# Attention, routed experts and a second attention on one core: the head of the first stage in another order, with filler matmuls

## The chip, the cores and the metric

One core of a Trainium2 chip runs one program: TensorE, VectorE, ScalarE and GpSimd compute, SyncE (SP) issues most of the DMAs. The metric is the device time of one execution in microseconds, lower is better; what stands for a kernel is the median of several executions.

## The reference, cut to what matters

Three stages in a row. The change touches the head of the first one only.

```
def _attn_ref(q, k, v, proj):                 # q, k, v: (2, 8, 768, 64), proj: (64, 6)
    scale = 1.0 / np.sqrt(D)
    q_bits = (np.einsum('bhsd,dk->bhsk', q, proj) > 0).astype(np.int64)
    k_bits = (np.einsum('bhsd,dk->bhsk', k, proj) > 0).astype(np.int64)
    powers = 2 ** np.arange(n_bits)
    q_bucket = np.sum(q_bits * powers, axis=-1)
    k_bucket = np.sum(k_bits * powers, axis=-1)
    mask = q_bucket[:, :, :, None] == k_bucket[:, :, None, :]
    scores = scale * np.matmul(q, k.transpose(0, 1, 3, 2))
    scores = np.where(mask, scores, -1000000000.0)
    scores = scores - np.max(scores, axis=-1, keepdims=True)
    attn = np.exp(scores)
    attn = attn / (np.sum(attn, axis=-1, keepdims=True) + 1e-09)
    return np.matmul(attn, v).astype(np.float32)

x = attention of all heads, (2, 768, 512)
x = _moe_ref(x, ...)      # each row through one of 8 experts, 512 -> 1024 -> 512
return _moe2_ref(x, ...)  # 4 experts that are causal attentions, the best 2 of each row
```

## The kernel before, in words

The first stage (`stage_a`) works on eight units, each a pair of heads of one batch, so that 128 partitions hold both heads or one head twice. For a unit it loads q and k transposed, makes their hash bits with a small matmul and a comparison, and builds wide operands `QM` and `KM`: rows 0 to 23 the bits, row 32 the row maxima of the scores (against ones on the side of k), rows 64 to 127 a rounded copy of q or k. One matmul of `KM` with `QM` so gives masked scores. What rounding lost is in `Q1` and `K1`, a second matmul.

Steps are small functions. Those of the head:

- `load(u, n)`: DMA of one head's q or k (n = 0 q of head 0, 1 k of head 0, 2 q of head 1, 3 k of head 1). In unit 0 it brings 64 partitions (192 KB), and `load2(n)` the same data to the other 64; in later units it brings 128 partitions (384 KB). `loadp(u, w)`: q (w = 0) or k (w = 1) of both heads, for the bits of units 1 to 7. `loadv(u)`: v. `proj`, `consts`: constants.
- `split(u, n)`: ScalarE rounds q or k into `QM`, `KM`. `split2(u, n)`: ScalarE rounds it into `Q1`, `K1`, and another engine subtracts to get the rest.
- `bits0(h, c, w)` (unit 0): matmul on TensorE, comparison on VectorE straight into `QM` or `KM`. `bits(u)` (other units): four matmuls, one comparison on VectorE; `qbits` and `kbits` then write the result into place on ScalarE.
- `mx(u, qh, n)`: one of twelve score matmuls of half qh, and its maximum on VectorE. `mneg`: the twelve to six. `mrow`: a transpose on TensorE, an eviction on VectorE and a DMA on SP (L287) that writes row 32.
- `score(u, x, h)`: two matmuls into one of three PSUM buffers `sc`, and the exp on ScalarE. `av`, `padd`, `sums`, `norm`, `rows1` to `rows3` follow. `warm(i, n)`: n filler matmuls whose result nobody reads. `fixed(i)`: memsets on GpSimd.

Each step is added to a plan with its dependences and costs of a planner (`at`, `ops`, in ns; those of bits of unit 0 are `("PE", 640, "S"), ("DVE", 660)`). The costs don't act when the kernel is built: `pl.run(ORDER_A)` calls the steps in the order of a list of numbers, and every engine and queue runs its instructions in just that order; waits come from the data. Eight fillers run ahead of the list. A PSUM pool `mx` of three buffers serves the bits, the maxima and the transposes.

The order written out, engine by engine, up to the first scores:

```
before
SP       load(0,1) proj proj load(0,2) load(0,3) load(0,0) load2(1) loadp(1,0) load(1,1) load2(3) consts load2(0)
         load(1,2) load(1,0) load2(2) loadp(1,1) load(1,3) mrow(0,0) loadv(0) loadp(2,1)
TensorE  bits0 x6, mx(0,0,.) x12, warm(1,2), bits(1), mrow(0,0), bits0 x2, warm(0,2), mx(0,1,.) x3,
         score(0,1,0) score(0,0,0) mx score(0,0,1) mx score(0,1,1)
VectorE  bits0 x6, mx x12, mneg, bits(1), mrow(0,0), bits0 x2, mx(0,1,.)
ScalarE  split(0,1) (0,3) (0,2) (0,0), split2(0,1) (0,0), split(1,1) (1,0), split2(0,3), split(1,3), split2(0,2),
         qbits(1,1), kbits x3, exp of score(0,1,0)
GpSimd   fixed(1) zeros fixed(0) identity, ones in pt, fill_table, subtractions of split2(0,1) (0,0) (0,3) (0,2)
```

Of the kernel before, what the change touches and what calls it, by code (L numbers as in the profile page):

```python
# [126 lines left out]
def stage_a(tc, ctx, g, q, k, v, pb):  # L127
    nc = tc.nc
# [101 lines left out]
    def split2(u, n):  # L230
        h, w = divmod(n, 2)
        X1 = (Q1, K1)[w][u % NB][:, h, :]
        x = st[u]["x"][w, h]
        lo = slice(64 * w, 64 * w + 64)
        nc.scalar.activation(X1, x, AF.Copy)
        e = nc.vector if u else nc.gpsimd
        e.tensor_sub(X1[lo], x[lo], X1[lo].bitcast(F32))
# [195 lines left out]

    def xout(kk, k):
        if kk + k == 0:
            sb.xt[0] = [sb.rp.tile([128, 4, CAP], F32R, name=f"x0{n}") for n in "hl"]
        h, l = (a[:, 2 * kk + k, :] for a in sb.xt[0])
        x = st["xt", kk][:, k, :]
        nc.scalar.activation(h, x, AF.Copy)
        nc.vector.tensor_sub(l, x, h.bitcast(F32))  # L440
# [15 lines left out]
    X = range(2)  # L456
    T = range(NKT)
    for n in X:
        add(proj, n, at=(-30.9, -29.4)[n], ops=dma(182), tail=900)
# [16 lines left out]
    for u in range(NU):  # L476
        b, p = units[u]
# [6 lines left out]
        for n in range(4):  # L484
            dep = [(f, u - 2, m) for f in ("split", "split2") for m in range(4)]
            dep += [("bits0", h, c, w) for w in X for c in X for h in X] if u == 2 else []
            add(load, u, n, at=o - 31 + 1.5 * n, ops=dma(1092 if u else 546), deps=dep + now(o - 31 + 1.5 * n) if u > 1 else [],
                tail=900)
            if u == 0:
                add(load2, n, at=-25 + n, ops=dma(546), deps=[("load", 0, n)], tail=900)  # L490
            add(split, u, n, at=o - 21 + n + 7 * (u == 1), ops=[("ACT", 740)], deps=[("load", u, n)] + seen)
            add(split2, u, n, at=o - 20 + n + 8 * (u == 1), ops=[("ACT", 735), ("DVE", 920, "p") if u else ("Pool", 1800, "p")],
                deps=[("load", u, n) if u else ("load2", n)] + used + [("mrow", 0, 0)] * (u == 1))
# [3 lines left out]
        for c in X:  # L497
            if u:
                add(loadp, u, c, at=o - 28 + c, ops=dma(1092), deps=([("bits", u - 1)] if u > 1 else []) + now(o - 28 + c) * (u > 1),
                    tail=900)  # L500
            else:
                for h in X:
                    for w in X:
                        add(bits0, h, c, w, at=-2 + h if c > w else -10 + 2.4 * h + .4 * (c + w), ops=[("PE", 640, "S"), ("DVE", 660)], bank="mx",
                            deps=[("load", 0, 2 * h + w), ("proj", 0), ("proj", 1)] + [("mneg", 0, 0)] * (c > w))
        if u:
            add(bits, u, at=o - 20 + 6 * (u == 1), ops=[("PE", 640, "Q"), ("DVE", 470)], bank="mx",
                deps=[("loadp", u, w) for w in X] + [("mneg", 0, 0)] + ([(f, u - 1, *x) for f, x in MOVES] if u > 1 else []))
# [8 lines left out]
        for qh in X:  # L517
            z = 2 * u + qh
            last = lambda f, n=2: [(f, *divmod(z - n, 2))] if z >= n else []
            for n in range(12):  # L520
# [4 lines left out]
                    + ([("mneg", u - 2, y) for y in X] if u > 1 else []), bank="mx")  # L525
# [4 lines left out]
            for kt in T:  # L530
# [7 lines left out]
                for h in X:  # L538
                    add(score, u, x, h, at=o + x + .4 * h, ops=[("PE", 349), ("ACT", 373)],
                        deps=[("mrow", u, qh)] + free + [("warm", i, 2) for i in X if u + qh == 0] + [(f, u, 2 * h + w) for f in ("split", "split2") for w in X] + bdep,  # L540
# [40 lines left out]
    u = NU - 1  # L581
# [1001 lines left out]
```

## Time and profile before

| | us |
|---|---|
| median of three executions | 607.95 (605.28 to 609.09) |
| the profiled execution, its own time | 608.14 |
| its span, first to last instruction | 606.4 |
| TensorE busy in the span | 579.6 (96%) |
| VectorE, ScalarE, GpSimd busy | 443.1, 369.8, 252.1 |

The first stage takes the span's first 250 us or so. Times in the profile count from the start of the span. A busy TensorE is not one at its peak, as its matmuls overlap. "A <- B" in a wait means that A's instruction waited for B's. The clock column is the granted clock of TensorE, 1.00 for 2.4 GHz and 0.50 for 1.2 GHz.

### The profile page before, as it was taken

What the parts mean: (1) busy time and instruction counts of PE and PEld (TensorE: products, weight loads), DVE (VectorE), ACT (ScalarE), POOL (GpSimd) and SP (SyncE); (2) the same over time, 40 slices, a digit from 0 to 9 for tenths busy, and PEclk for the clock granted to TensorE, in tenths of its full rate; (3) what the DMA queues carried; (4) which work ended last, traced back from release to release, by engine and by line L of the source; (5) the groups of instructions that cost most, each with busy time, mean ns of one, the idle gap of its engine ahead of it and who ended that gap; (6) DMA issues with size and microseconds to landing.
All of it is one profiled execution on the core that took longest, in us unless ns stands there. A gap on an engine that the chain in (4) does not pass through costs nothing. (4 is left out here: it accounts for less than half of the span.)

```text
span 606.4 us, 9769 instructions
## 1 busy us (share of the span) xinstructions
PE 579.6 (96%) x3537; PEld 448.8 (74%) x3537; DVE 443.1 (73%) x853; ACT 369.8 (61%) x676; POOL 252.1 (42%) x256
## 2 busy tenths in 40 slices
PE   8999989999899999899999999999989999998995
PEld 3556657767576675798898998997969878787573
DVE  6699888988889798756656776755444576787872
ACT  4999878989695476154545545544537565554541
POOL 7696577686767784620000000000044024653840
PEclk8999999999999999899999999999999999999998
DMA  8535347265425415247656757665555010210222
GB/s 230 206 130 174 119 151 261 75 225 157 166 62 174 120 56 183 89 138 250 242 176 248 243 198 242 220 233 174 177 166 155 18 28 15 66 27 2 54 105 104
DMA packets 53718, 88.81 MB, mean 146 GB/s; under 512 B 3860, under 2 KB 26512, under 8 KB 53408
## 3 DMA queue, kind: packets, MB, share of 16 engines
q1 hardware_dynamic: 51712, 81.78, 41.3%
q0 software_dynamic: 1952, 6.34, 3.3%
q8 instruction: 29, 0.48, 0.4%
q14 instruction: 25, 0.20, 0.1%
HBM read 66.18 MB, written 20.26 MB: 143 GB/s over the span
## 5 line engine op out<-in xcount | busy, mean ns | idle before, releaser
L320 POOL TENSOR_TENSOR acc<-acc,pt 128x768 f32<-128x768 f32 x56 | 110.6, 1977 | 43.0 <-ACT pt L298 40.6
L274 DVE TENSOR_REDUCE m<-mp 128x1 f32<-128x384 f32 x192 | 96.4, 548 | 10.0 <-PE mp L273 9.2
L298 ACT ACTIVATE pt<-sc 128x384 f32<-128x384 f32 x192 | 85.5, 486 | 24.1 <-PE sc L297 21.1
L1079 POOL DMA_INDIRECT xg<-ys,slot x12 | 12.2, 1018 | 193.4 <-DVE wl L1049 185.7
L850 DVE TENSOR_TENSOR wlo<-wraw,whi 128x1024 fp32r<-128x1024 f32 x64 | 76.3, 1231 | 12.3 <-ACT whi L849 12.2
L307 PE MATMUL av<-pt,vt 128*64 128x385 f32 (+1 forms) x384 | 70.7, 493 | 0.0
L273 PE MATMUL mp<-km,qm 128*128 128x384 f32 x192 | 65.3, 379 | 5.4 <-DVE m L274 3.6
L849 ACT ACTIVATE whi<-wraw 128x1024 fp32r<-128x1024 f32 x64 | 64.4, 1053 | 9.0 <-DMA wraw<-in_w_dram 5.3
L295 PE MATMUL sc<-qm,km 128*128 128x384 f32 x192 | 67.6, 352 | 1.2 <-ACT pt L298 0.6
L297 PE MATMUL sc<-q,k 128*128 128x384 f32 x192 | 64.6, 336 | 0.0
L889 PE MATMUL hp<-xth,whi 128*128 128x256 f32 x224 | 63.0, 281 | 1.7 <-PEq L1017 1.7
L890 PE MATMUL hp<-xtl,whi 128*128 128x256 f32 x224 | 62.9, 281 | 0.0
L891 PE MATMUL hp<-xth,wlo 128*128 128x256 f32 x224 | 62.8, 280 | 0.0
L273 PEld LDWEIGHTS mp<-km,qm 128*128 128x128 f32 x192 | 35.6, 192 | 25.1 <-DVE m L274 10.6
L907 PE MATMUL yp<-whi,hh 128*128 128x512 f32 x128 | 51.5, 402 | 0.0
L908 PE MATMUL yp<-wlo,hh 128*128 128x512 f32 x128 | 50.4, 393 | 0.0
L909 PE MATMUL yp<-whi,hl 128*128 128x512 f32 x128 | 50.3, 393 | 0.0
L307 PEld LDWEIGHTS av<-pt,vt 128*64 128x64 f32 x384 | 25.4, 136 | 32.1 <-issue 28.8
L894 ACT ACTIVATE hh<-hp 128x512 fp32r<-128x512 f32 x32 | 19.1, 598 | 45.0 <-PE hp L891 44.9
L1281 POOL TENSOR_TENSOR cp<-cp,cp 128x384 f32<-128x384 f32 (+2 forms) x50 | 39.5, 812 | 17.0 <-PE cav L1273 16.1
L889 PEld LDWEIGHTS hp<-xth,whi 128*128 128x128 f32 x224 | 42.1, 188 | 2.4 <-issue 2.1
L895 DVE SCALAR_TENSOR_TENSOR hl<-hp,hh 128x512 fp32r<-128x512 f32 x32 | 22.0, 688 | 28.4 <-ACT hh L894 28.4
(263 smaller groups left out, 1387.6 us busy)
## 6 DMA issues: line engine op xcount, KB each, us to landing
wraw<-in_w_dram SPq DMA_DIRECT2D x32, 1024.0 KB
xs<-zt SPq DMA_DIRECT2D x13, 512.0 KB
x<-in_k_dram SPq DMA_DIRECT2D x14, 384.0 KB
x<-in_q_dram SPq DMA_DIRECT2D x14, 384.0 KB
xsb<-xs SPq DMA_DIRECT2D x7, 512.0 KB
ys<-ysb SPq DMA_DIRECT2D x7, 512.0 KB
vt<-in_v_dram SPq DMA_DIRECT2D x8, 384.0 KB
xp<-in_q_dram SPq DMA_DIRECT2D x7, 384.0 KB
```

The source lines that it names most:

```text
L273: nc.tensor.matmul(mp, QM[i][:, o:o + 128], KM[i][:, h * S + c * HS:h * S + (c + 1) * HS], start=True, stop=True)
L274: nc.vector.tensor_reduce(s["m"][:, qh, h, t, c:c + 1], mp, axis=AX.X, op=ALU.max)
L295: nc.tensor.matmul(sc, KM[i][:, h * S + kt * 128:h * S + kt * 128 + 128], QM[i][:, (2 * qh + h) * HS:(2 * qh + h + 1) * HS], start=True, s ...
L297: nc.tensor.matmul(sc, K1[i][:, h, ks], Q1[i][:, h, qs], start=False, stop=True)
L298: nc.scalar.activation(PT[(u * 12 + x) % NPB][:, h, :HS], sc, AF.Exp, scale=SCALE)
L307: nc.tensor.matmul(s["av", qh][64 * h:64 * h + 64, :HS + 1 - qh], s["v"][:, h, kt, :], P[:, h, :HS + 1 - qh], start=kt == 0, stop=kt == NK ...
L320: (nc.vector if u == NU - 1 else nc.gpsimd).tensor_add(s["acc", qh], p, P)
L849: nc.scalar.activation(hi[:, s], r[:, s], AF.Copy)
L850: nc.vector.tensor_sub(lo[:, s], r[:, s], hi[:, s].bitcast(F32))
L889: nc.tensor.matmul(p[:, f2, :], hi, xh[:, k, :], start=k == 0, stop=False)
L890: nc.tensor.matmul(p[:, f2, :], hi, xl[:, k, :], start=False, stop=False)
L891: nc.tensor.matmul(p[:, f2, :], lo, xh[:, k, :], start=False, stop=k == 3)
```

## The change

The list ORDER_A has a new beginning; its last 945 steps are the same steps in the same order. The first unit's eight loads and the constants are issued first. The transpose of the first row of maxima (`mrow(0,0)`) and its DMA come before the second unit's bits, and the second unit's loads come behind that DMA on SP. Thirteen steps `hwarm` put filler matmuls between the bits of the first unit (three, three) and between its first twelve maxima (one each). `warm(0)` and `warm(1)` have three fillers instead of two. Two of the first unit's four subtractions go from GpSimd to VectorE, behind the row.

```
after
SP       load(0,1) proj proj load(0,0) load(0,3) load(0,2) load2(1) load2(0) load2(3) load2(2) consts
         mrow(0,0) loadp(1,0) loadp(1,1) load(1,0) load(1,1) load(1,2) load(1,3) loadv(0) loadp(2,1)
TensorE  bits0(0,0,1) (0,1,1), 3 fillers, bits0(0,0,0) (1,0,1) (1,1,1), 3 fillers, bits0(1,0,0),
         mx(0,0,0) filler mx(0,0,1) filler ... mx(0,0,11), mrow(0,0), 6 fillers, bits(1), bits0 x2, mx(0,1,.) x3,
         score(0,1,0) score(0,0,0) mx score(0,0,1) mx score(0,1,1)
VectorE  bits0 x6, mx x12, mneg, mrow(0,0), subtractions of split2(0,3) (0,2), bits(1), bits0 x2, mx(0,1,.)
ScalarE  split(0,1) (0,0) (0,3) (0,2), split2(0,1) (0,0) (0,3) (0,2), split(1,1) (1,0) (1,3),
         qbits(1,1), kbits x3, exp of score(0,1,0)
GpSimd   fixed(0) identity, ones in pt, fixed(1) zeros, subtractions of split2(0,1) (0,0), fill_table
```

The code of it, cut to its core:

```
-        e = nc.vector if u else nc.gpsimd
+        e = nc.vector if u or h else nc.gpsimd
         e.tensor_sub(X1[lo], x[lo], X1[lo].bitcast(F32))
...
+    def hwarm(i, n):
+        warm(i, n)
+
...
+    for i, n in enumerate((3, 3) + (1,) * 11):
+        add(hwarm, i, n, at=-8, ops=[("PE", 213 * n)], deps=[("mx", 0, 0, i - 4)] if i > 3 else [], bank="sc")
...
-            add(load, u, n, at=o - 31 + 1.5 * n, ops=dma(1092 if u else 546), deps=dep + now(o - 31 + 1.5 * n) if u > 1 else [],
+            add(load, u, n, at=o - 31 + 1.5 * n, ops=dma(1092 if u else 700), deps=dep + now(o - 31 + 1.5 * n) if u > 1 else [("load2", y) for y in range(4)] * u,
                 tail=900)
             if u == 0:
-                add(load2, n, at=-25 + n, ops=dma(546), deps=[("load", 0, n)], tail=900)
+                add(load2, n, at=-25 + n, ops=dma(700), deps=[("load", 0, y) for y in range(4)], tail=900)
...
-                            deps=[("load", 0, 2 * h + w), ("proj", 0), ("proj", 1)] + [("mneg", 0, 0)] * (c > w))
+                            deps=[("load", 0, 2 * h + w), ("proj", 0), ("proj", 1)] + [("mrow", 0, 0)] * (c > w))
         if u:
             add(bits, u, at=o - 20 + 6 * (u == 1), ops=[("PE", 640, "Q"), ("DVE", 470)], bank="mx",
-                deps=[("loadp", u, w) for w in X] + [("mneg", 0, 0)] + ([(f, u - 1, *x) for f, x in MOVES] if u > 1 else []))
+                deps=[("loadp", u, w) for w in X] + [("mrow", 0, 0)] + ([(f, u - 1, *x) for f, x in MOVES] if u > 1 else []))
...
+                    + ([("hwarm", n + 1, 1)] if u + qh == 0 and n else []), bank="mx")
...
-        add(warm, i, 2, at=-3 + .3 * i, ops=[("PE", 850)], deps=[("mx", 0, 0, 11)], bank="sc")
+        add(warm, i, 3, at=-3 + .3 * i, ops=[("PE", 640)], deps=[("mx", 0, 0, 11)], bank="sc")
```

The dependences of the plan (`deps`) only say which orders are allowed; the order is the list's.

## Rows read from the trace of the kernel before

**Rows 1.** Busy times by stretch: engines, then granted clock, DMA share, GB/s.

```profile
20.00:30.00 10.00, 9.32 (x48) 6.68 (x47) 8.12 (x18) 9.83 (x17) 7.42 (x8) 1.00 0.66 238
```

**Rows 2.** Waits from 22 to 255 us: total, times, longest.

```profile
ACT pt L298 <- PE sc L297: 21.1, 40, 2.0
...
PEld sc L295 <- DMA qm<-mr: 0.9, 1, 0.9
```

**Rows 3.** Timeline of ScalarE: start, duration, instruction, idle before and releaser.

```profile
18.12 0.84 ACT L227 ACTIVATE km<-x 64x768 fp32r<-64x768 f32 x1 [0.71 <-DMA x<-in_k_dram]
18.99 0.84 ACT L235 ACTIVATE q<-x 128x768 fp32r<-128x768 f32 x1
19.86 1.03 ACT L258 ACTIVATE qm<-bt,cstt 24x768 fp32r<-24x768 f32 x1
...
22.82 2.19 ACT L298 ACTIVATE pt<-sc 128x384 f32<-128x384 f32 x5
```

**Rows 4.** Timeline of the SP queue: start and duration of the issue.

```profile
11.58 0.33 SPq L164 DMA_DIRECT2D x<-in_k_dram  x1
19.07 0.88 SPq L287 DMA_DIRECT2D qm<-mr  x1
20.00 0.39 SPq L184 DMA_DIRECT2D vt<-in_v_dram  x1
...
22.60 0.91 SPq L164 DMA_DIRECT2D x<-in_k_dram  x2
```

**Rows 5.** Waits of the SP queue in the first 30 us.

```profile
SPq L287 <- DVE mr L286: 7.1, 1, 7.1
```

**Rows 6.** Timeline of VectorE.

```profile
5.30 1.32 DVE L253 TENSOR_SCALAR km<-bp,cstt 32x384 fp32r<-32x384 f32 x2 [4.15 <-PE bp L251]
...
9.68 5.64 DVE L274 TENSOR_REDUCE m<-mp 128x1 f32<-128x384 f32 x12
15.36 0.17 DVE L280 TENSOR_REDUCE mn<-m 128x6 f32<-128x12 f32 x1
...
18.72 0.27 DVE L286 TENSOR_SCALAR mr<-mtp 6x128 fp32r<-6x128 f32 x1
```

**Rows 7.** Timeline of TensorE in the head.

```profile
17.20 1.00 PE L243 MATMUL bp<-xp,pbt 128*32 128x384 f32 x4 [0.22 <-DMA xp<-in_k_dram]
18.13 0.27 PE L284 MATMUL mtp<-ident,mn 128*6 128x128 f32 x1
...
23.33 0.44 PE L295 MATMUL sc<-qm,km 128*128 128x384 f32 x1 [0.63 <-ACT pt L298]
```

**Rows 8.** Busy times by stretch, with the granted clock, around the first maxima.

```profile
10.90:17.60 6.70, 6.48 (x16) 2.69 (x18) 4.59 (x11) 3.36 (x4) 2.86 (x3) 0.50 0.99 310
```

**Rows 9.** Busy times by stretch, read for the last column, GB/s.

```profile
17.00:18.00 1.00, 0.80 (x4) 0.19 (x4) 0.00 (x0) 0.41 (x1) 0.51 (x1) 0.72 0.27 101
20.00:21.00 1.00, 0.96 (x5) 0.44 (x3) 1.00 (x3) 0.99 (x2) 1.00 (x1) 1.00 0.01 3
21.00:28.00 7.00, 6.37 (x34) 5.12 (x33) 5.54 (x13) 6.89 (x12) 5.87 (x7) 1.00 0.93 336
34.00:36.00 2.00, 2.00 (x12) 1.99 (x12) 1.68 (x4) 1.97 (x5) 1.87 (x2) 1.00 1.03 403
```

**Rows 10.** Busy times and granted clock where the first stage ends.

```profile
252.00:258.00 6.00, 5.31 (x29) 4.85 (x30) 3.33 (x17) 0.60 (x2) 4.15 (x9) 0.72 0.23 89
254.00:256.00 2.00, 2.00 (x9) 1.64 (x8) 0.94 (x8) 0.00 (x0) 0.72 (x1) 0.50 0.34 131
```

**Rows 11.** Timeline of TensorE near 252 us and near the end.

```profile
252.69 0.50 PE L428 MATMUL sc<-q,qm 128*128 128x256 f32 x2 [2.01 <-DVE q L423]
...
258.13 1.90 PE L1455 MATMUL sc<-onesb 128*128 128x512 bf16 x8
...
598.54 0.63 PE L1330 MATMUL cop<-wh,cxl 128*128 128x512 f32 x1
598.97 0.63 PE L1328 MATMUL cop<-wh,cah 128*128 128x512 f32 x1
```

More of the change, by code (lines that the diff above doesn't have):

```diff
@@ L486, in stage_a @@
             dep += [("bits0", h, c, w) for w in X for c in X for h in X] if u == 2 else []
-            add(load, u, n, at=o - 31 + 1.5 * n, ops=dma(1092 if u else 546), deps=dep + now(o - 31 + 1.5 * n) if u > 1 else [],
+            add(load, u, n, at=o - 31 + 1.5 * n, ops=dma(1092 if u else 700), deps=dep + now(o - 31 + 1.5 * n) if u > 1 else [("load2", y) for y in range(4)] * u,
                 tail=900)
             if u == 0:
-                add(load2, n, at=-25 + n, ops=dma(546), deps=[("load", 0, n)], tail=900)
+                add(load2, n, at=-25 + n, ops=dma(700), deps=[("load", 0, y) for y in range(4)], tail=900)
             add(split, u, n, at=o - 21 + n + 7 * (u == 1), ops=[("ACT", 740)], deps=[("load", u, n)] + seen)
-            add(split2, u, n, at=o - 20 + n + 8 * (u == 1), ops=[("ACT", 735), ("DVE", 920, "p") if u else ("Pool", 1800, "p")],
-                deps=[("load", u, n) if u else ("load2", n)] + used + [("mrow", 0, 0)] * (u == 1))
+            add(split2, u, n, at=o - 20 + n + 8 * (u == 1), ops=[("ACT", 735), ("DVE", 920, "p") if u or n > 1 else ("Pool", 1800, "p")],
+                deps=[("load", u, n) if u else ("load2", n)] + used + [("mrow", 0, 0)] * (u == 1) + [("mneg", 0, 0)] * (u == 0 and n > 1))
         add(loadv, u, at=o - 20, ops=dma(1092), deps=[("av", u - 3, x) for x in range(12)] if u > 2 else now(o - 20) if u > 1 else [],
@@ L498, in stage_a @@
             if u:
-                add(loadp, u, c, at=o - 28 + c, ops=dma(1092), deps=([("bits", u - 1)] if u > 1 else []) + now(o - 28 + c) * (u > 1),
+                add(loadp, u, c, at=o - 28 + c, ops=dma(1092), deps=([("bits", u - 1)] + now(o - 28 + c) if u > 1 else [("load2", y) for y in range(4)]),
                     tail=900)
@@ L524, in stage_a @@
                     + ([("bits0", h, qh, 0), ("bits0", h, n % 2, 1)] if u == 0 else [])
-                    + ([("mneg", u - 2, y) for y in X] if u > 1 else []), bank="mx")
+                    + ([("mneg", u - 2, y) for y in X] if u > 1 else [])
+                    + ([("hwarm", n + 1, 1)] if u + qh == 0 and n else []), bank="mx")
             e = o - 6 + 6 * qh if u else 3.1 * qh - 3.2
@@ L539, in stage_a @@
                     add(score, u, x, h, at=o + x + .4 * h, ops=[("PE", 349), ("ACT", 373)],
-                        deps=[("mrow", u, qh)] + free + [("warm", i, 2) for i in X if u + qh == 0] + [(f, u, 2 * h + w) for f in ("split", "split2") for w in X] + bdep,
+                        deps=[("mrow", u, qh)] + free + [("warm", i, 3) for i in X if u + qh == 0] + [(f, u, 2 * h + w) for f in ("split", "split2") for w in X] + bdep,
                         bank="sc")
```

88 rows, old and new, of the table ORDER_A are left out of this document.

## The prediction

> **What bounds the kernel now.** I read five views, in this order. First the busy times by stretch: from 20 to 30 us ScalarE is busy 9.83 of 10 us and TensorE 9.32 [rows 1], so once the attention stage runs there is no room in which a late start could be made good. Second, the waits from 22 us to the end of that stage: engines wait for each other (ScalarE for the scores, 21.1 us in all), and the only wait of a computing engine for a DMA is 0.9 us for a row of maxima; none is for a load of q or k [rows 2]. A delay that all engines have after the head therefore reaches the end whole. Third, ScalarE's timeline: the last part of the second unit that is read from memory is copied at 18.12 (it waited 0.71 us for the DMA of k), one more copy of the first unit follows at 18.99, the second unit's bits at 19.86, and the first exp only at 22.82 [rows 3]. The head ends at this exp: TensorE has three buffers for scores, and its fourth score pair, at 23.33, waits for it [rows 7]. Fourth, the SP queue, which issues in program order: the second unit's last load leaves at 11.58, then the queue stands 7.1 us before the DMA of the first row of maxima, because that needs VectorE's result, and only at 20.00 does the next load leave [rows 4, 5]. Fifth, why the row is late: VectorE has the maxima ready at 15.53 (15.36 + 0.17) [rows 6], but the transpose that makes the row stands on TensorE behind the second unit's bits, which wait for k until 17.20; it runs at 18.13 and the DMA leaves at 19.07 [rows 4, 7].
>
> **The change part by part.** What may be gained: the row no longer stands behind the second unit's bits. What is paid: the second unit's six loads now stand behind the row's DMA on SP, and ScalarE needs three of them, the last one among them, before the first exp.
>
> *The first row of maxima.* VectorE's first piece still starts at 5.30, as the first load and the two constants keep their places. Six evictions of bits at 0.66 (two take 1.32) are followed by twelve maxima in 5.64, 0.47 each [rows 6]. The fillers, three each before the third and the sixth piece of bits, cost at the full clock at most 0.24 each (eight in 1.90) [rows 11], 0.7 a time. With 0.64 for a piece of bits on TensorE (the cost in the code): the third is done at 5.74 + 0.7 + 0.64 = 7.1 where VectorE was free at 6.6, the sixth at about 9.7 where VectorE was free at 9.2. Two gaps of about 0.5 to 0.65, so the evictions end at 10.45 and the maxima at 16.1; before they ended at 15.3. The loads that come sooner gain nothing here, since each of the pieces had its data by then. Between maxima, one filler and one maximum's matmul take 0.24 x (1 + 384/512) = 0.42 at the full clock, under VectorE's 0.47: no cost. The row then needs the reduction 0.17, the transpose 0.27, the eviction 0.27 and some 0.1 for each handover [rows 6, 7]: the DMA leaves at 17.05 instead of 19.07. That is the whole gain, 2.0 us. It can't be much more: with no gap the evictions and maxima take 4.0 + 5.64 from 5.30, and the DMA leaves at 15.9.
>
> *The second unit's loads.* All six wait on SP until the row's DMA is issued. That takes 0.88 [rows 4], so the first goes out at 17.95. Before, a load issued at 20.00 had moved next to nothing by 21.0 (3 KB in that us), and from 21 to 28 us six loads of 0.393 MB, 2.36 MB, were moved at 336 GB/s, 2.35 MB [rows 4, 9]. That stretch had gaps between the issues (20.00 to 23.5); issued back to back at 0.46 (two in 0.91 [rows 4]) the rate should be nearer to the 403 GB/s of 34 to 36 us [rows 9]. Six loads take 7.0 us by the one and 5.85 by the other; I take 6.2, nearer to the back-to-back rate. First data at 17.95 + 1.15 = 19.1, last at 25.3. Before, data stopped some 0.27 us after 17 us (101 KB at about 380 GB/s) and the copy that waited for it started at 18.12 [rows 3, 9], so I add 0.85: the copy starts at 26.15. The first unit's copies are all done by then, so the second unit's bits follow at once, at 27.0, where they ran at 19.86 [rows 3]: **+7.15 us**. From there to the first exp ScalarE's order is unchanged (2.96 us from the one row to the other), so it starts at 30.0 instead of 22.82. The bounds: DMA at 15.9, 5.85 us of transfer and a tail of 0.7 give +4.9; with 7.0 us and a row 0.5 later, +8.5.
>
> The Trainium skill puts a DMA at about 2.0 us fixed plus bytes over 436 GB/s ("DMA: Bandwidth & Descriptors", Anatomy of one DMA; a fit for GpSimd's queue). For one stream of these bytes that would be an estimated 7.4 us from issue to landing where my rows give 8.2, and a time 0.8 us lower. The same page's Rules for kernel authors say to issue early and wait late, which this change does the other way round for the second unit.
>
> *What TensorE does meanwhile.* The second unit's bits stand ahead of all scores on TensorE and need the first two loads, landed at about 19.1 + 2.0 + 0.85 = 22. So TensorE is idle from about 18.3 (the six fillers behind the row) to 22, then runs the bits, seven matmuls and three score pairs, and is idle again from about 26.5 until 30.5. Before, after an idle time of 2.0 us that ended at 252.7, the granted clock was at 0.50 in 254 to 256 [rows 10, 11]; at that level a 512-column matmul takes 0.43 (two starts, 598.54 and 598.97) instead of at most 0.24 [rows 11]. If the clock is low where the scores restart, TensorE, which has no room there, loses up to half of that stretch: 1.7 us for a drop as long as that one (a mean of 0.72 over 6 us is 3.4 us at 0.50 [rows 10]), 0 if it stays high or falls in the idle time. I take **+0.5**.
>
> The Trainium skill describes a kernel whose waits for DMA let the clock fall at every round ("TensorE: Matmul & The Clock Gate", HAM oscillation). By it the fall would be sure and the time 1.2 us above my sum.
>
> *The rest.* Two of the four subtractions of the first unit move from GpSimd to VectorE behind the row, where VectorE waits for the second unit's bits anyway until 23; the first unit's last copies move ahead on ScalarE, which waits until 24 anyway; the memsets change places on GpSimd, whose first result is needed at about 9.7 and ready at 5: nothing on the path. If the loads did not cover them, the subtractions would be about 2 us on VectorE. The v load is seventh, lands at about 27.2 and is needed at about 32.5. The remaining 945 steps keep their order.
>
> **Sum.** 608.14 us (the profiled execution: its span 606.4 and 1.7 around it) + 7.15 + 0.5 = **615.8 us**. The median shown, 607.95, lies 0.2 below that execution.
>
> **The rivals.**
> *The first row is slowed by its own fillers.* Before, the clock was at 0.50 from 10.9 to 17.6 [rows 8], through most of the maxima. If it is so again, a matmul of 384 columns and a filler take 0.32 + 0.43 = 0.75 instead of 0.47, and the twelve maxima 9.0 instead of 5.64; where half of them see the low clock, 1.7 more. For it: the low stretch is there in the trace. Against it: the fillers are just what keeps TensorE denser than before. All that follows shifts by it: 617.5 to 619.
> *The loads come faster or part of the delay is made good.* With the lower bounds above, +4.9 gives 613.0; with 2 us made good by waits that I have overlooked in the stage, 611 to 613.5.
> *The loads are not held back, and the 2.0 us are kept* (the other side). If the SP queue let the loads go when they are reached in the list, before the row's DMA, they would start at about 8 us, behind the first unit's 1.6 MB, and all be there by about 16, as before by 18. The first exp would then follow the row: 608.14 - 2.0 = 606.1. It decides when the sixth load has landed by about 17.9, two us before the bits' 19.86. Against it speaks the queue's own row: 7.1 us of standing before the row's DMA with loads queued behind it [rows 5], and loads that leave in just the order of the list. That would also be the case where the change doesn't do what I read in it.
>
> **How the numbers follow.** Chances: 0.50 for my sum (613.5 to 617.5), 0.22 for slow maxima, 0.20 for the smaller delay, 0.08 for no delay. The predicted time is the first one's, 615.8. The range leaves out the last case and the end of the second: 611.0 to 620.0. About 1%, 6.1 us, is what a measurement of this kernel can tell from no change; three runs lay between 605.28 and 609.09. Slower by more than that means over 614.0: nearly all of slow maxima and somewhat under 0.9 of the first case with the scatter of the runs, less a little: 0.69. Faster needs under 601.9, which no case gives: 0.03. The rest is 0.28.
>
> **What would show it.** In the changed trace: on SP a load of k or q leaving right behind the row's DMA at about 18, none of the second unit before; ScalarE waiting some 9 to 13 us for loads of k and q, with the last wait ending near 26; the first exp near 30; TensorE with two idle stretches of 3 to 4 us before 31; the row's DMA near 17. From then on every landmark (the last exp of the stage, the first expert's matmul) some 7 to 8 us later than before. I am wrong if the second unit's loads are issued before the row, if ScalarE's copies precede 22 us, or if the shift shrinks on the way to the end.

## The result and the profile after

The changed kernel takes 617.81 us (median of four executions, 615.78 to 620.1) against 608.52 for the kernel before: ratio 1.0144, 95% interval 1.0103 to 1.0184. Measured once more beside the kernels of the experiments, it takes 618.45 (four executions, 614.99 to 621.83) against 607.65, ratio 1.0171 (1.011 to 1.0231). The forecast was 615.8, within 611 to 620, slower. The execution that was profiled took 615.78 against 608.14, with a span of 614.0 against 606.4.

The row's DMA leaves earlier, as it was meant to, and the second unit's loads go out behind it. The SP queue of the changed kernel (timeline, then its longest wait), to be read against [rows 4, 5]:

```profile
7.53 0.62 SPq L205 DMA_DIRECT2D cstt<-in_cst_dram  x1
17.24 0.88 SPq L287 DMA_DIRECT2D qm<-mr  x1
18.17 0.39 SPq L179 DMA_DIRECT2D xp<-in_q_dram  x1
...
20.50 0.57 SPq L164 DMA_DIRECT2D x<-in_k_dram  x1
21.11 0.53 SPq L184 DMA_DIRECT2D vt<-in_v_dram  x1
...
SPq L287 <- DVE mr L286: 9.0, 1, 9.0
```

The queue stands 9.0 us before the row's DMA with nothing in flight for the second unit; the sixth load leaves at 20.50 where it left at 11.58. VectorE shows why the row is no sooner than 17.24 (its timeline, against [rows 6]): two gaps, 0.84 and 0.18, where TensorE runs fillers ahead of the third and the sixth piece of bits, then the twelve maxima at the old pace.

```profile
5.54 1.32 DVE L253 TENSOR_SCALAR km<-bp,cstt 32x384 fp32r<-32x384 f32 x2 [4.40 <-PE bp L251]
7.70 0.66 DVE L253 TENSOR_SCALAR qm<-bp,cstt 32x384 fp32r<-32x384 f32 x1 [0.84 <-PE bp L251]
...
9.87 0.67 DVE L253 TENSOR_SCALAR qm<-bp,cstt 32x384 fp32r<-32x384 f32 x1 [0.18 <-PE bp L251]
10.57 5.66 DVE L274 TENSOR_REDUCE m<-mp 128x1 f32<-128x384 f32 x12
```

ScalarE pays (its timeline, against [rows 3]): it is done with the first unit at 12.2, stands 13.44 us until k of the second unit has landed, once more 0.37 for the last load, and starts the first exp at 31.38 instead of 22.82.

```profile
11.36 0.85 ACT L235 ACTIVATE q<-x 128x768 fp32r<-128x768 f32 x1
25.64 0.84 ACT L227 ACTIVATE km<-x 64x768 fp32r<-64x768 f32 x1 [13.44 <-DMA x<-in_k_dram]
...
27.57 0.84 ACT L227 ACTIVATE km<-x 64x768 fp32r<-64x768 f32 x1 [0.37 <-DMA x<-in_k_dram]
28.43 1.02 ACT L258 ACTIVATE qm<-bt,cstt 24x768 fp32r<-24x768 f32 x1
...
31.38 1.21 ACT L298 ACTIVATE pt<-sc 128x384 f32<-128x384 f32 x3
32.95 0.49 ACT L298 ACTIVATE pt<-sc 128x384 f32<-128x384 f32 x1 [0.36 <-PE sc L297]
33.91 0.49 ACT L298 ACTIVATE pt<-sc 128x384 f32<-128x384 f32 x1 [0.47 <-PE sc L297]
```

The last two rows show the second, smaller loss: ScalarE now waits for scores. Busy times by stretch, with granted clock, DMA share and GB/s in the last three columns, against [rows 9, 10]:

```profile
20.00:22.00 2.00, 0.79 (x4) 0.14 (x4) 0.00 (x0) 0.00 (x0) 0.00 (x0) 0.91 1.14 341
22.00:24.00 2.00, 1.39 (x6) 0.19 (x4) 0.00 (x0) 0.00 (x0) 0.00 (x0) 0.50 0.78 229
24.00:26.00 2.00, 1.86 (x6) 0.19 (x4) 0.67 (x2) 0.36 (x1) 0.00 (x0) 0.50 1.04 410
...
34.00:36.00 2.00, 2.00 (x9) 1.16 (x7) 1.38 (x3) 1.96 (x4) 1.35 (x1) 0.68 0.00 0
...
252.00:258.00 6.00, 5.80 (x47) 4.90 (x47) 5.39 (x30) 1.24 (x4) 1.59 (x3) 1.00 0.22 82
```

The clock is at 0.50 from 21.6 us until 35.3, over the first 3.9 us of exps, and the loads have a slack stretch of 229 GB/s at 22 to 24 us.

How the delay goes on can be read from landmarks. The row of `mneg` (sixteen in the stage: count, shortest, median and longest in ns, first and last start) in the kernel before and in the changed one:

```profile
L280 DVE TENSOR_REDUCE mn<-m x16: 125/155/166, 15.4 to 216.6; 128x6 f32<-128x12 f32 x16
```

```profile
L280 DVE TENSOR_REDUCE mn<-m x16: 126/156/168, 16.3 to 226.6; 128x6 f32<-128x12 f32 x16
```

The first exp is 8.6 us late, the last `mneg` 10.0. Nothing is made good from the first exp to there. Behind it 2.4 us come back in this pair of executions (the spans differ by 7.6): the kernel before had its clock down in 252 to 258 us (0.72 [rows 10]), the changed one nowhere between its last `mneg` and its last 20 us. What follows the last `mneg` goes with that clock in all fourteen profiles: 386.5 to 389.0 us in the seven without such a fall, 388.6 to 390.5 in the five with one or two falls of 3.4 us, 391.8 and 392.8 in the two with 10 us at the low level. Whether the changed kernel has fewer of these falls than the kernel before, or had so by chance, stays open. The medians differ by 9.3.

### The profile page after: what moved, and what is told of

It reads as the page before. It is cut to its first block, busy times and chain, and to the rows that moved or that the text cites. A ratio compares the mean times of both kernels' runs of the same rounds, so it can differ in the third digit from the quotient of the medians.

```text
span 614.0 us, 9808 instructions
## 1 busy us (share of the span) xinstructions
PE 583.2 (95%) x3556; PEld 450.8 (73%) x3556; DVE 443.7 (72%) x855; ACT 370.1 (60%) x676; POOL 250.4 (41%) x254
## 5 line engine op out<-in xcount | busy, mean ns | idle before, releaser
L1287 POOL TENSOR_TENSOR cp<-cp,cp 128x384 f32<-128x384 f32 (+2 forms) x50 | 39.5, 812 | 16.9 <-PE cav L1279 15.2
L896 PEld LDWEIGHTS hp<-xtl,whi 128*128 128x128 f32 x224 | 42.1, 188 | 0.2
```

The costliest lines, as they stand in the source:

```text
L896: nc.tensor.matmul(p[:, f2, :], hi, xl[:, k, :], start=False, stop=False)
```

## The experiments

Four theories. A: the second unit's loads, held on SP behind the row's DMA, are the loss. B: the fillers, or the clock, are. C: the two subtractions on VectorE delay the second unit's bits. D, against a part of the prediction: the row was not what ended the head of the kernel before, so its 2 us are worth nothing.

The kernels change the order by a small function ahead of the run:

```
    def moved(order, steps, mark):              # these steps right ahead of that one
        keys = list(pl.items)
        ids = [keys.index(s) for s in steps]
        order = [n for n in order if n not in ids]
        at = order.index(keys.index(mark))
        return order[:at] + ids + order[at:]
```

What all of them showed, by profile: when the row's DMA left on SP, when the first exp and the last `mneg` started (in parentheses how much later than in the kernel before), and the time as a ratio to the kernel before.

| kernel | loads held | row's DMA | first exp | last mneg | ratio (95%) |
|---|---|---|---|---|---|
| before | 0 | 19.07 | 22.82 | 216.6 | |
| row ahead of the bits alone (e3) | 0 | 16.99 | 22.69 (-0.1) | 216.6 (0) | 1.001 (0.9987 to 1.0033) |
| loads ahead, no fillers (e8) | 0 | 16.95 | 23.76 (0.9) | 217.5 (0.9) | 1.0013 (0.998 to 1.0046) |
| e8, bits sooner (e10) | 0 | 17.11 | 23.41 (0.6) | 217.5 (0.9) | 1.0009 (0.9985 to 1.0034) |
| e8, bits among the maxima (e9) | 0 | 19.13 | 23.07 (0.3) | 217.2 (0.5) | 0.9999 (0.9966 to 1.0032) |
| loads ahead (e1) | 0 | 22.47 | 27.88 (5.1) | 221.6 (5.0) | 1.0011 (0.9977 to 1.0045) |
| two held, no fillers (e12) | 2 | 16.51 | 25.42 (2.6) | 219.2 (2.6) | 1.0056 (1.0025 to 1.0087) |
| two held (e6) | 2 | 17.09 | 25.82 (3.0) | 219.6 (3.0) | 1.0126 (1.0072 to 1.018) |
| no fillers (e2) | 6 | 16.42 | 30.21 (7.4) | 225.8 (9.2) | 1.0148 (1.0098 to 1.0198) |
| changed | 6 | 17.24 | 31.38 (8.6) | 226.6 (10.0) | 1.0144 (1.0103 to 1.0184) |
| changed, again (e13) | 6 | 23.76 | 37.98 (15.2) | 231.8 (15.2) | 1.0171 (1.011 to 1.0231) |
| last two exchanged (e4) | 6 | 22.62 | 36.16 (13.3) | 230.4 (13.8) | 1.0141 (1.0093 to 1.0189) |
| more fillers in the idle time (e5) | 6 | 17.91 | 31.87 (9.1) | 227.1 (10.5) | 1.0207 (1.0116 to 1.0298) |
| e2, first unit's exps first (e11) | 6 | 17.98 | 23.21 (0.4) | 232.1 (15.5) | 1.0231 (1.018 to 1.0281) |

**Loads ahead of the row's DMA (e1).**

```
+    order = moved(ORDER_A, [("loadp", 1, 0), ("loadp", 1, 1), ("load", 1, 0), ("load", 1, 1), ("load", 1, 2), ("load", 1, 3)], ("fixed", 0))
```

> The changed kernel with one thing undone: the second unit's six loads are issued right behind the constants, ahead of the first row's DMA; the fillers, the row ahead of the bits and the moved subtractions stay. Theory A (the loads held on SP behind the row's DMA are the cost): ScalarE's wait of 13.4 us for k shrinks to below 6 us, the second unit's bits follow the two subtractions on VectorE, the first exp starts near 22.7 instead of 31.4, and the time is that of the kernel before within 2 us (606 to 610). Theory B (the fillers, or the low clock that follows them, are the cost): the time stays above 614. Theory C (the two subtractions on VectorE delay the bits): a rest of 1 to 2 us against the kernel before stays.

608.55 us against 606.63: the loss is gone, as far as the interval tells, with the loads back in front, while all fillers and the moved subtractions stay. Five of its ten executions lie between 605.9 and 607.4, as the kernel before does; the others reach up to 615.29. ScalarE's wait for k fell to 3.65 us. A holds, B is out as the main cause. The first exp of the profiled execution (612.38) was not at 22.7, though, but at 27.88, since here the row's DMA left only at 22.47 and the second unit's bits stand behind it; more on that below. ScalarE of this kernel:

```profile
15.94 0.84 ACT L227 ACTIVATE km<-x 64x768 fp32r<-64x768 f32 x1 [3.65 <-DMA x<-in_k_dram]
...
24.92 1.03 ACT L258 ACTIVATE qm<-bt,cstt 24x768 fp32r<-24x768 f32 x1 [6.21 <-DVE bt L245]
```

**No fillers among bits and maxima (e2).**

```
     def hwarm(i, n):
-        warm(i, n)
+        pass
```

> The changed kernel without the seventeen fillers among the first bits and maxima (the six behind the row stay). Theory A: the maxima end 0.6 to 1.2 us sooner, the row's DMA and the loads behind it leave as much sooner, the first exp comes near 30.5 instead of 31.4; the time stays 6.5 to 9 us above the kernel before. Theory B: the time falls to within 2 us of the kernel before. Should the clock be at 0.50 during the maxima as in the kernel before, VectorE still sets their pace at 0.47.

Row at 16.42, first exp at 30.21, 616.25 us: still 9.6 us above the kernel before. As A expected, the fillers are 0.8 us of the row and 1.2 us of the first exp in this pair of profiles.

**The row ahead of the second unit's bits, in the kernel before (e3).**

```
+    order = moved(ORDER_A, [("mrow", 0, 0)], ("bits", 1))
```

> The kernel before with one part of the change: the transpose and DMA of the first row of maxima come ahead of the second unit's bits; loads, fillers and subtractions as before. Theory A, in the form of the prediction (the row is worth what its DMA gains): the row's DMA leaves at 16.4 instead of 19.07 and the time falls by 2 us or more. Theory D (the row was not last: ScalarE's copies and bits of the second unit set the first exp at 22.8 in any case): the row's DMA leaves as much sooner, the first exp stays at 22.8 within 0.3, and the time stays within 1 us of the kernel before.

The row's DMA leaves 2.1 us sooner, and the first exp moves by 0.1. From the SP queue and ScalarE of this kernel:

```profile
16.99 0.88 SPq L287 DMA_DIRECT2D qm<-mr  x1
```

```profile
18.86 0.84 ACT L235 ACTIVATE q<-x 128x768 fp32r<-128x768 f32 x1
19.73 1.03 ACT L258 ACTIVATE qm<-bt,cstt 24x768 fp32r<-24x768 f32 x1
...
22.69 2.19 ACT L298 ACTIVATE pt<-sc 128x384 f32<-128x384 f32 x5
```

ScalarE works from one copy to the next up to the exp as before. D holds: the row was early enough already.

**The last two held loads exchanged (e4).**

```
+    order = moved(ORDER_A, [("load", 1, 3)], ("load", 1, 2))
```

> The changed kernel with the last two of the six held loads exchanged: k of the second head, for which ScalarE waits last, is fifth and q of the second head, which ScalarE needs only after the first exps, is sixth. Theory A: ScalarE's last wait for k ends one load sooner, the first exp comes 0.9 to 1.0 us sooner (30.4), and the time falls by about as much (0.5 to 1.5 us). Theory B: the same as the changed kernel, first exp at 31.4.

The profiled execution had a late row (22.62), so it is read from there. The first exp came 13.54 us behind the row's DMA instead of 14.14: 0.6 us, not 0.95. ScalarE of this kernel shows where the rest went: the wait for the last load is gone, and the copies now follow each other, bound by the fourth load ahead of them.

```profile
30.89 0.84 ACT L227 ACTIVATE km<-x 64x768 fp32r<-64x768 f32 x1 [18.73 <-DMA x<-in_k_dram]
31.63 0.82 ACT L227 ACTIVATE qm<-x 64x768 fp32r<-64x768 f32 x1
32.36 0.82 ACT L227 ACTIVATE km<-x 64x768 fp32r<-64x768 f32 x1
```

The time, 617.1, can't tell a change that small.

**More fillers in the idle time (e5).**

```
+    add(warm, 8, 14, at=0, ops=[], bank="sc")
+    order = moved(ORDER_A, [("warm", 8, 14)], ("bits", 1))
```

> The changed kernel with fourteen more fillers behind the six that follow the row, in the 3 us in which TensorE stands idle before the second unit's bits. If the low clock from 21 us on is a cost of its own (0.8 us between the first exp and the next 5 us, where ScalarE waits 0.36 and 0.47 for scores): the granted clock stays at 1.00 past 22 us, the first exp stays near 31.4 (the loads set it), ScalarE's waits for scores behind it go, and what follows at 38 us comes 0.8 us sooner than in the changed kernel; the time falls by 0.5 to 1. If it isn't: no difference. If the fillers are still running when the bits' loads land, the bits are up to 0.3 us later, without effect on ScalarE.

The clock stays up through the first idle time, but falls at 33.3 us, 0.9 us after TensorE's second idle time (28.3 to 32.4), and the low stretch now lies wholly on the scores and exps (busy times and clock of this kernel):

```profile
24.00:31.00 7.00, 3.43 (x17) 1.95 (x15) 4.37 (x8) 4.47 (x6) 0.00 (x0) 1.00 1.02 401
31.00:35.00 4.00, 2.61 (x10) 2.31 (x10) 1.20 (x3) 3.87 (x9) 1.38 (x1) 0.79 0.41 158
35.00:40.00 5.00, 5.00 (x22) 2.77 (x22) 3.42 (x8) 4.36 (x7) 1.11 (x2) 0.83 0.00 0
```

ScalarE waits 0.52 and 0.62 us for scores a little later, and from the first exp to the last `mneg` the delay grows by 1.4 us, as in the changed kernel. Nothing is won; the expected 0.5 to 1 us did not come, as the clock fell behind the later idle time instead. Its four executions lie between 616.86 and 628.6; only the one at 620.69 was profiled, and why two lie above 625 is open.

**Two of six held (e6, e12).** In e6 four of the six loads are ahead of the row's DMA; e12 is the same without fillers.

```
+    order = moved(ORDER_A, [("loadp", 1, 0), ("loadp", 1, 1), ("load", 1, 0), ("load", 1, 1)], ("fixed", 0))
```

> The changed kernel with four of the second unit's six loads ahead of the first row's DMA and two (q and k of the second head) behind it. Theory A by dose: the last load ScalarE needs is then second behind the row, it lands about 5 us behind the DMA's issue instead of 10.3; the first exp comes near 26.2 to 26.6 instead of 31.4 where the row's DMA leaves at 17.2, and the time lies 3 to 4.5 us above the kernel before (610 to 612). Any theory in which the fillers or the subtractions matter: no such step between e1 and the changed kernel.

> Two of the six loads held behind the row's DMA (as in e6), without the seventeen fillers. Theory A by dose, freed of the executions in which the fillers run at the low clock: the first exp near 25.5, 2.5 to 3 us behind the kernel before, and all executions within 609 to 613. If e6's executions at 616 came from something else than slow fillers: again several near 616.

The heads come out as A has it by dose: 3.0 and 2.6 us behind the kernel before. ScalarE of e12:

```profile
21.61 0.85 ACT L227 ACTIVATE km<-x 64x768 fp32r<-64x768 f32 x1 [4.14 <-DMA x<-in_k_dram]
...
25.42 2.19 ACT L298 ACTIVATE pt<-sc 128x384 f32<-128x384 f32 x5
```

The times of e6 did not: its profiled execution took 611.79, four others 615.8 to 617.1. That is why e12 was run: without fillers the ten executions lie between 608.75 and 613.09, median 610.93, 3.3 us above the 607.65 of the kernel before. Without fillers the steps by dose are thus 1.0013, 1.0056, 1.0148 for none, two and six held.

**Loads ahead, no fillers (e8), bits sooner (e10), bits among the maxima (e9): looking for a gain.** e8 is e1 without the seventeen fillers; e10 has also the subtractions back on GpSimd and the second unit's bits ahead of the six fillers; e9, with the subtractions on GpSimd too, puts these bits ahead of the ninth maximum, and on ScalarE `qbits` and `kbits` of the second unit ahead of its `split` steps.

```
+    order = moved(order, [("bits", 1)], ("warm", 0, 3))                               # e10
+    order = moved(order, [("bits", 1)], ("mx", 0, 0, 8))                              # e9
+    order = moved(order, [("qbits", 1, 1), ("kbits", 1, 0, 0), ("kbits", 1, 1, 1), ("kbits", 1, 1, 0)], ("split", 1, 1))
```

> The kernel with the loads ahead (e1) without the seventeen fillers among the first bits and maxima. If the fillers cost where TensorE's clock is still low when the kernel begins (e1: the third piece of bits came 2.1 us late, the row's DMA at 22.5): the row's DMA leaves between 16 and 17.2, the first exp starts near 22, and the time is 0.5 to 3 us below that of e1. If the fillers earn something through the clock, it is above that of e1.

> Loads ahead of the row's DMA, no fillers among bits and maxima (as in e8), all four subtractions on GpSimd, and the second unit's bits directly behind the row's transpose, ahead of the six fillers. In e8 the bits' comparison on VectorE came at 20.16, held by six fillers at the low clock (2.8 us) and before that by two subtractions. Here it should come near 18.6 (low clock) or 18.0, the first exp near 22.1 or 21.5 instead of 22.8 in the kernel before: 0.7 to 1.3 us gained in the head, a ratio of 0.997 to 1.0, at the edge of what five rounds can tell. If it isn't the order of the head but the clock that decides the rest, the ratio is 1.0 or above.

> A version that the runs point to: loads ahead of the row's DMA, no fillers among bits and maxima, all four subtractions on GpSimd, the second unit's bits on TensorE and VectorE ahead of the ninth maximum, and their copies on ScalarE in the time in which it waited for k (12 to 16 us). If ScalarE's order up to the first exp is what ends the head: the row's DMA leaves near 17.0 (one eviction of 0.56 more ahead of it), the row lands near 19, the first exp starts near 19.7 instead of 22.8, and the time is 2 to 3.5 us below the kernel before (603 to 605). If the first exp isn't what sets the rest, no difference from the kernel before.

None beats the kernel before: 1.0013, 1.0009 (607.14 against 607.65, interval 0.9985 to 1.0034), and e9 0.9999 (0.9966 to 1.0032). Each time another link came last. In e8 it is the fillers behind the row (six in 2.8 us at the low clock), which hold the second unit's bits on TensorE. The two subtractions on VectorE are done by then: VectorE waits 1.31 us for the bits before it compares them, so C is worth nothing here, and in e1, where VectorE goes from the subtractions to the comparison without a gap, at most 0.2 us. VectorE of e8:

```profile
20.16 0.56 DVE L245 TENSOR_SCALAR bt<-bp 128x384 f32<-128x384 f32 x1 [1.31 <-PE bp L243]
```

In e10 ScalarE is ready at 21.9 and waits 1.50 us for scores, as the same fillers, now ahead of the last two pieces of the first unit's bits, take 2.28 us on TensorE. TensorE's timeline, and ScalarE's:

```profile
18.09 2.28 PE L1471 MATMUL sc<-onesb 128*128 128x512 bf16 x6
20.29 0.83 PE L251 MATMUL bp<-x,pbt 64*32 64x384 f32 x4
```

```profile
23.41 2.40 ACT L298 ACTIVATE pt<-sc 128x384 f32<-128x384 f32 x5 [1.50 <-PE sc L297]
```

In e9 the bits took 2.19 us on TensorE at the low clock in the middle of the maxima, the row's DMA left at 19.13, and the first exp came at 23.07 instead of 19.7, as ScalarE waited 1.50 us for scores there too.

**The first unit's exps ahead of the second unit's steps, loads still held (e11).**

```
+    order = moved(ORDER_A, [("bits", 1), ("split", 1, 1), ("split", 1, 0), ("split", 1, 3), ("split", 1, 2),
+                            ("qbits", 1, 1), ("kbits", 1, 0, 0), ("kbits", 1, 1, 1), ("kbits", 1, 1, 0), ("qbits", 1, 0), ("kbits", 1, 0, 1),
+                            ("loadp", 2, 1), ("loadp", 2, 0)], ("mx", 1, 0, 5))
```

> The changed kernel without the seventeen fillers, the second unit's loads still held behind the row's DMA, but the second unit's steps (its bits, copies and bits' copies, and the loads that need its bits done) moved behind the first eight exps of the first unit on all engines. If the loss is that the first unit's exps stand in ScalarE's order behind a wait for the second unit's loads: the first exp starts near 20, ScalarE's wait for k is split, some 2 to 3 us of it left at about 24, and the time lies 3 to 5 us above the kernel before instead of 9 (611 to 613). If the loss is the late loads as such, whatever stands behind them: no better than the changed kernel without fillers (616.3).

It did not help: 621.3 us, 1.0231 (1.018 to 1.0281). The first exp comes at 23.21, not near 20, but without waiting for the second unit: ahead of it stand the six fillers at the low clock (2.76 us). Then the stage stops twice. Waits of this kernel from 10 to 60 us:

```profile
PE mp L273 <- ACT qm L258: 6.7, 1, 6.7
...
PE av L307 <- DMA vt<-in_v_dram: 3.8, 1, 3.8
```

v is the seventh load behind the row's DMA, so the first unit's product with v waits for it, the exps behind that come late, ScalarE reaches the second unit's copies late, and the second unit's maxima wait for these. So the exps in ScalarE's order are not the only ones who wait: with the second unit's steps put eight exps later the late loads were a loss too. Other distances were not tried.

**The changed kernel again (e13).**

> The changed kernel once more, unaltered, beside the others on one chip. In e1 and e4 the first pieces of bits took twice as long (clock still low at 5 us) and the row's DMA left at 22.5 instead of 17.2. If that is a matter of the single execution: the changed kernel shows either head, row's DMA at 17.2 to 17.9 or near 22.5, and its times spread over 4 to 5 us (615 to 621), ratio 1.013 to 1.017.

Its eight executions fall into two groups: 614.99, 615.32, 615.78, 616.14, and 619.47, 620.1, 621.58, 621.83. One of each was profiled. TensorE in the one that took 615.78:

```profile
4.68 1.47 PE L251 MATMUL bp<-x,pbt 64*32 64x384 f32 x4
6.08 0.82 PE L1461 MATMUL sc<-onesb 128*128 128x512 bf16 x3
```

and in the one that took 621.58:

```profile
4.73 2.77 PE L251 MATMUL bp<-x,pbt 64*32 64x384 f32 x4
7.43 1.46 PE L1461 MATMUL sc<-onesb 128*128 128x512 bf16 x3
...
14.33 0.69 PE L273 MATMUL mp<-km,qm 128*128 128x384 f32 x1
14.82 0.65 PE L1461 MATMUL sc<-onesb 128*128 128x512 bf16 x1
14.91 0.88 PE L273 MATMUL mp<-km,qm 128*128 128x384 f32 x1
```

The same instructions take nearly twice as long: this is the low level of the clock, from the first bits until about 20 us, with a maximum every 0.77 us. The row's DMA leaves at 23.76. (The clock column reads 1.00 up to the first record of the trace, whatever the level; the durations tell it.)

## Why the prediction was right, step by step

**The mechanism.** It went as the prediction had it: the SP queue issues in order, the six loads wait for the row's DMA, ScalarE waits for the last of them, the first exp ends the head and the delay reaches the end. e8, e12 and e2 show it by dose without the fillers (0, 2 and 6 loads held), e1 with them. Two signs are off in size: ScalarE waited 13.8 us for the loads, where 9 to 13 were forecast, and TensorE's second idle time is 1.34 us, where 3 to 4 were.

**The row's DMA: 17.05 forecast, 17.24 measured**, with two gaps on VectorE, 1.0 us in sum where some 1.2 was worked out, and a first piece at 5.54 instead of 5.30. In half of the executions it isn't so, see the rival below.

**The six loads: mis-sized by 1.2 us.** From the first issue to the copy that waits for the last load, 17.95 to 26.15 was forecast, 8.2 us; it took from 18.17 to 27.57, 9.4. The term that was too small is the transfer: I took 6.2 us, nearer to the rate without gaps between issues, and data ran from about 19.2 to 26.6, 7.4 us, slower than even the 7.0 of [rows 9]. The 403 GB/s were taken from the middle of a run of loads, and such a run starts slowly: from the first data on, the six profiles with six held loads moved 276 to 313 GB/s in the first 4 us and 364 to 385 in the next 3. What slows the start wasn't tried. The Trainium skill's fixed time and rate ("DMA: Bandwidth & Descriptors", Anatomy of one DMA), an estimated 7.4 us from issue to landing where 9.4 us were measured up to the copy, is further off than the rows' 8.2.

**The first exp: 30.0 forecast, 31.38 measured**, +8.6 instead of +7.15, by the loads' 1.2 and the row's 0.2.

**The clock: +0.5 forecast, 1.4 measured.** It fell at 21.6, behind an idle time of TensorE from 18.1 to 21.2, and lay over the first 3.9 us of exps. The Trainium skill describes such falls behind waits for DMA ("TensorE: Matmul & The Clock Gate", HAM oscillation), and the trace agrees with 0.50 from 21.6 to 35.3. The delay grew by 0.8 us up to ScalarE's copy at 38.74 and by 1.4 up to the last `mneg`. Over the profiles that growth goes with the low clock behind the first exp: 1.8 us for 4.6 us at 0.50 in e2, 1.4 for 3.9 in the changed kernel, 1.4 for 3.4 in e5, 0.4 for 1.5 in e4, and between -0.1 and 0.3 in the eight where the clock was up by then (e1, e3, e6, e8, e9, e10, e12, e13; e11 waits for loads besides). So it is a cost only where the low stretch meets the scores, and the 1.4 lies within the bounds of 0 to 1.7. The short second idle time belongs to it: 1.34 us at the low clock, 4.12 in e5, where TensorE worked towards it at 1.00.

**The sum** of 7.65 met 7.64 in the profiled pair by accident: 8.6 + 1.4 - 2.4, the last one a low clock behind the first stage that the kernel before had in this execution and the prediction had no term for. The medians, 9.3 and 10.8 us apart, hold the two terms that were too small and the slow heads; that they lie inside the range is luck in part, as the eight executions fall into the two groups of e13, and three of the upper four lie above 620. Two sums on record do not come out: by its own terms the lower bound of the delay is +5.5 and not +4.9 (1.15 of row, 0.35 of transfer and 0.15 of tail off 7.15), and 0.22 with under 0.9 of 0.50 stays under the 0.69 for slower.

**The rival of the slow maxima was not a rival but half of the executions.** I gave it 0.22 and 617.5 to 619; the group lies at 619.5 to 621.8. Its price was too small because I put the low clock on the maxima alone, as in [rows 8]; in e13 the six pieces of bits and the fillers between them run at it too, and the row is 6.5 us late. That this separates the two groups is shown for the two profiled executions; of the other six it is argued from their times, as it is for e6's. Late heads (row's DMA later than 22 us) were seen in three of the six profiles with fillers between bits and maxima (e1, e4, e13) and in none of the eight without. The long low stretch comes without these fillers too: in e11 all twelve matmuls of the six pieces took 5.71 us where e10 needs 4.43, the clock was low until 20.1, and the row's DMA left at 17.98, 1 to 1.5 us later than in e2, e8, e10 and e12 (16.42 to 17.11). So with the fillers the row pays 5 to 6.5 us for a low clock that costs 1 to 1.5 without them. TensorE of e11:

```profile
4.73 5.71 PE L251 MATMUL bp<-x,pbt 64*32 64x384 f32 x12
```

Whether they also make it more frequent, three of six profiles against one of eight can't tell.

**The rival of the kept 2.0 us was wrong in its size.** I had loads that are not held at 606.1. With them in front the time is that of the kernel before (e1, e8), and e3 shows why: the row's 2.1 us bring nothing by themselves, since ScalarE's copies and the second unit's bits set the first exp. The "whole gain, 2.0 us" was a gain of one wait that was not the last. It did no harm to the sum, as that followed ScalarE.

**The part hidden at no cost:** the subtractions on VectorE cost nothing while the loads are late, as forecast: VectorE waits 5.35 us for the second unit's bits behind them. With the loads in front they would cost "about 2 us on VectorE" by the prediction; they cost nothing in e8 and at most 0.2 in e1, as TensorE's fillers hold the bits as long.

## What to carry to other kernels

A wait put into an in-order DMA queue holds every load behind it: before moving a small dependent DMA forward, list what is queued behind it and who needs the last of those. A step that is made sooner is worth only what the other inputs of its user allow; here ScalarE's row of copies, unbroken from 18.12 to the first exp [rows 3], told that the early row of maxima would bring nothing. And fillers meant to raise the clock are work on the path while it is still low; put into the first of two idle times, as in e5, they only moved the low stretch behind the second.

## What was not expected of the hardware

The level of the clock at the first matmuls differs between executions of one kernel: the first four instructions of bits took 1.47 us in one and 2.77 in the other, behind the same eight fillers, and with fillers in the path that moved the head by 6.5 us. The first clock record of the trace, at which the durations fall to those of 1.00, stands at 3.9 to 6.2 us in ten of the fourteen profiles and at 16.8 to 20.1 in the other four (e1, e4, e11, e13). The loads of the second unit, issued back to back, ran at 341, 229 and 410 GB/s in three stretches of 2 us; the slow start shows in every profile with six held loads, and none shows its reason.
